# Two value steps in one run, side work at the steps between: the full-attention layers of a four-layer attention stack

## The chip, the cores and the metric

The kernel runs on one core of a Trainium2 chip. The metric is the device time of one execution in microseconds. The engines are named as in the profile: PE is TensorE (matmuls; PEld its weight loads), ACT is ScalarE, DVE is VectorE, POOL is GpSimd, SP is SyncE, from whose queue the kernel issues its DMAs.

## What is computed

Four attention layers follow each other, each with a layer norm before it and a residual sum behind it. Layers 0 and 2 look back over a window of 256 positions; layers 1 and 3 are full attention over all 2048 positions, without a mask. There are 32 heads of 16 elements.

```python
B, S, D = 1, 2048, 512
H = 32; Dh = D // H
def _B_ref(x, wqkv, wo):
    qkv = (x @ wqkv).reshape(B, S, 3, H, Dh).transpose(2, 0, 3, 1, 4)
    q, k, v = qkv[0], qkv[1], qkv[2]
    scores = jnp.einsum("bhqd,bhkd->bhqk", q, k) * Dh ** -0.5
    p = _softmax(scores, axis=-1)
    o = jnp.einsum("bhqk,bhkd->bhqd", p, v)
    return o.transpose(0, 2, 1, 3).reshape(B, S, D) @ wo

x = A_x
x = x + _A_ref(_layernorm(x), A_wqkv, A_wo)   # the same within a window of 256
x = x + _B_ref(_layernorm(x), B_wqkv, B_wo)
x = x + _A_ref(_layernorm(x), A_wqkv, A_wo)
x = x + _B_ref(_layernorm(x), B_wqkv, B_wo)
```

## The kernel before

**A step of a full layer.** The queries are cut into four chunks of 512 (c), the heads into eight groups of four (qd), the keys into sixteen tiles of 128 (j). `attn_full` (line 685) does one key tile of one head group and one chunk per step. It calls `exps` (line 642) twice, once for each pair of heads. A call takes a score buffer `s` in PSUM, fills it by two 64-row matmuls that stand side by side in the array (line 649), and has ACT take the exponential of its 128x1024 elements into a buffer `e` (line 653). There are three score buffers (pool `ps_s`, line 200) and six buffers `e` (`EB`, line 34), so six exponentials, or three steps, can be held. What I call a score tile below is one such call; a step has two.

**The values of a step** are four matmuls (line 693), one for each head, with the probabilities `e` as the moving operand and 17 columns of values (16 and a one, which gives the softmax's sum) as the stationary one. They are float32, and the profile shows each of them as two, so a step's values are eight matmuls there, in two groups of four that run side by side in the array's columns. They add up in one PSUM bank, `acc[0]`, over the sixteen steps. `attn_full` doesn't issue them itself: it hands them out as a function, which `attention` puts into the queue `pvq` and issues later with `flush` (line 656).

```python
def flush(n):
    while len(pvq) > n:
        spent(1.0)
        for f in pvq.popleft():
            f()
```

**Behind the last step of a head group** the function `epilogue` (line 591) hangs on the same queue entry: DVE copies `acc[0]` to SBUF (line 599), DMAs take it to DRAM, and two later pieces (`run_late`, line 634) take the reciprocals of the sums and normalise. The first values of the next head group write `acc[0]` again and wait for that copy.

**Side work** is everything that isn't the attention itself: projections for this layer and the next (line 385, 12 matmuls of 512 columns per output tile), the output projection, transposes for the layer norm (line 429). In a full layer it has the other bank, `acc[1]` (`bank`, line 374), and `mms` (line 380) hands it out matmul by matmul. The class `Side` (line 794) puts it in: `Side.step` (line 838) issues pieces until the share due by then is done, at most about 3 us of planned time a call, and stops behind the end of a chain of matmuls. The share due is counted in steps, and a work is taken only when a planned clock (`clock`, moved by `spent`, line 213) says that its inputs are there.

**Order.** PE follows the order in which the program is written out (`manual_schedule`), and `attention` (line 869) writes it. DVE, ACT, POOL and SP follow a scheduler. In a full layer before the change, every step writes its scores, and then `flush(2)` the values of the step two before; odd steps add side work behind them. Two steps make a unit: scores, values, scores, values, side. There are 256 units in each full layer. In a window layer every step does all three.

Of the kernel before, what the change touches and what calls it, by code (L numbers as in the profile page):

```python
# [189 lines left out]
def fast_path(ctx, tc, flag, a_x, a_wqkv, a_wo, b_wqkv, b_wo, out):  # L190
# [22 lines left out]
    def spent(us):  # L213
        clock[0] += us
        return us
# [306 lines left out]
    def settle(all_=True):  # L522
        while pend and (all_ or pend[0][0] <= clock[0]):
            pend.pop(0)[1]()
# [109 lines left out]
    def run_late(done=False):  # L634

        while late and (done or late[0][0] <= 0):
            late.popleft()[1]()
        for x in late:
            x[0] -= 1
# [16 lines left out]
# [5 lines that stand above are left out]
# [208 lines left out]
    def attention(l, works):  # L869

        win = l % 2 == 0
        PH["full"] = not win
        load = load_win if win else load_full
        for t in range(NHT if l == 3 else 1):
            for c in range(NQ):
                qds = range(2 * t, 2 * t + 2) if l == 3 else range(NQD)
                ops = load(l, c, qds[0])
                sd = Side((3 if win else NT) * len(qds) // (1 if win else 2), works[t * NQ + c], works[t * NQ + c + 1])
                k = 0
                for qd in qds:  # L880
                    nxt = load(l, c, qd + 1) if qd + 1 in qds else None
                    a = acc[qd % 2 if win else 0]
                    began = clock[0]
                    for f in (attn_win if win else attn_full)(l, c, qd, *ops, a):
                        clock[0] = max(clock[0], began + (2.4 if win else 1.8))
                        began = clock[0]
                        pvq.append([f])
                        flush(2)
                        run_late()
                        if win or k % 2:  # L890
                            sd.step()
                        if win:
                            settle(False)
                        k += 1
                    pvq[-1].append(lambda l=l, c=c, qd=qd, a=a: epilogue(l, c, qd, a, False))
                    ops = nxt
                sd.finish()
                if not win:
                    settle()
        flush(0)  # L900
        run_late(True)
        PH["full"] = False
# [122 lines left out]
    for l in range(4):  # L1025
        if l % 2 == 0:
            attention(l, works[l] + [tails[l][1:]])
            all_of(tails[l], lasts[l])
            key_shift(l + 1, 0 if l else None)
            all_of(lasts[l], works[l + 1][0])  # L1030
        else:
            attention(l, works[l] + [works[2][0] if l == 1 else [O3(3, 3)]])
# [38 lines left out]
```

## Time and profile before

| | |
|---|---|
| median of 3 runs | 2972.41 us (2970.57 to 2975.87) |
| profiled execution, its time | 2971.72 us |
| its span | 2970.0 us |
| mean granted clock of TensorE | 0.979 |
| PE busy | 2740.4 us |
| ACT busy | 2400.6 us |
| DVE busy | 904.0 us |
| POOL busy | 561.7 us |
| exponentials (line 653), all layers | 2432 instructions, 2244.0 us busy |
| values of the full layers (line 693) | 8192 matmuls in the profile, 1078.5 us busy |
| scores, all layers (line 649) | 5504 matmuls, 797.1 us busy |

A group's row gives line, engine, operation, output <- inputs, shapes and count; then busy time and the mean of one in ns; then the idle time of its engine before these instructions, and what ended it. A row of a timeline gives the start and the duration in us, the same description, and in brackets the idle time before. A row of the table by stage gives the stretch, then busy time and count of PE, PEld, DVE, ACT and POOL, the granted clock, the share of the DMA engines and GB/s. A row of the waits gives who waited for whom, the total in us, how often, and the longest. Matmuls overlap and their ends are modelled: the distance from one start to the next tells more than the duration.

### The profile page before, as it was taken

To read this page: it belongs to the slowest core of one execution; us is meant where nothing else is said; L and a number is where in the kernel's file an instruction comes from. 1 tells how busy PE (TensorE), PEld (TensorE's weight loads), DVE (VectorE), ACT (ScalarE), POOL (GpSimd) and SP (SyncE) were. 2 spreads that over 40 slices of the span, in tenths; PEclk is the share of its full clock that TensorE was granted. 3 is DMA by queue.
4 is the path that set the end of the run, shared out by engine and by line. 5 is a ranking of instruction groups with operands and counts; after the bars stand their busy time and mean duration, and the time that the engine had idled before them with its cause. 6 is when DMAs were issued, how large, how long until landed. Compare 5 with 4: busy or idle time off the path is not lost.

```text
span 2970.0 us, 52024 instructions
## 1 busy us (share of the span) xinstructions
PE 2740.4 (92%) x20314; PEld 745.7 (25%) x20314; DVE 904.0 (30%) x1914; ACT 2400.6 (81%) x2703; POOL 561.7 (19%) x1127
## 2 busy tenths in 40 slices
PE   6778889899999999999999888899999999999996
PEld 3233333321122212212212333332112211121111
DVE  7656444401113112111212455631222222222112
ACT  3454555389999999999998666639999999999996
POOL 2456564100000000000002566600000000000000
PEclk8898999999999999999999999999999999999998
DMA  6575775532223233222222756542343334333331
GB/s 212 188 227 189 237 228 172 186 107 100 77 92 104 76 115 102 92 86 93 93 102 94 228 187 184 166 135 86 127 130 123 114 126 134 123 120 122 122 114 66
DMA packets 291409, 399.35 MB, mean 134 GB/s; under 512 B 70352, under 2 KB 173264, under 8 KB 283856
## 3 DMA queue, kind: packets, MB, share of 16 engines
q1 hardware_dynamic: 291152, 395.92, 41.0%
q8 instruction: 161, 2.64, 0.4%
q14 instruction: 96, 0.79, 0.1%
HBM read 263.19 MB, written 131.60 MB: 133 GB/s over the span
## 4 chain that ended last, share of the span: by engine, by line
PE 65%; ACT 10%; DMA 10%; DVE 7%; issue 4%; POOL 2%; SPq 1%; ACTq 0%; DVEq 0%; POOLq 0%
PE acc L693 26%; PE s L649 18%; ACT e L653 9%; PE acc L385 9%; PE pq L385 4%; DMA r<-rcp 4%; PE pv L385 3%; DMA rcp<-lt 2%; PE acc L725 2%; PE po L385 2%; DMA scr<-oe 1%; POOL wr L326 1%; DMA x<-in_A_x_dram 1%; POOL w L331 1%; DVE o L626 1%
## 5 line engine op out<-in xcount | busy, mean ns | idle before, releaser
L653 ACT ACTIVATE e<-s 128x1024 f32<-128x1024 f32 (+2 forms) x2432 | 2244.0, 1113 | 173.5 <-PE s L649 156.7
L693 PE MATMUL acc<-e,vt 128*17 128x512 f32 x8192 | 1078.5, 598 | 2.8 <-DVE oe L599 2.7
L649 PE MATMUL s<-qt,kt 64*128 64x512 f16 (+3 forms) x5504 | 797.1, 356 | 88.1 <-ACT e L653 16.6
L649 PEld LDWEIGHTS <-kt 64*128 64x128 f16 x5504 | 219.1, 94 | 953.0 <-issue 928.5
L718 POOL TENSOR_SCALAR_AFFINE_SELECT e<-e 128x256 f32<-128x256 f32 x512 | 229.0, 454 | 186.4 <-ACT e L653 185.5
L599 DVE COPY oe<-acc 128x512 f32<-128x512 f32 x128 | 88.0, 687 | 510.4 <-PE acc L693 449.2
L629 POOL TENSOR_TENSOR oh<-o,oh 128x512 f16<-128x512 f32 x32 | 37.1, 1159 | 1076.6 <-DVE oh L628 1060.9
L693 PEld LDWEIGHTS acc<-e,vt 128*17 128x17 f32 x8192 | 136.4, 95 | 349.0 <-issue 322.9
L715 POOL TENSOR_SCALAR_AFFINE_SELECT e<-e 128x256 f32<-128x256 f32 x448 | 195.4, 442 | 151.1 <-ACT e L653 148.1
L385 PE MATMUL pq<-xc,w 128*128 128x512 f16 x816 | 198.3, 397 | 20.0 <-DVE dx L567 5.3
L725 PE MATMUL acc<-e,vt 128*17 128x384 f32 (+2 forms) x2816 | 203.7, 396 | 5.4 <-POOL e L715 5.3
L385 PEld LDWEIGHTS <-w 128*128 128x128 f16 x1152 | 106.5, 100 | 254.5 <-issue 161.7
L626 DVE TENSOR_TENSOR o<-o,r 128x512 f32<-128x512 f32 x64 | 51.9, 811 | 352.4 <-DMA r<-rcp 344.7
L385 PE MATMUL po<-wo,oh 128*128 128x512 f16 x444 | 113.5, 409 | 39.1 <-DVE oh L628 19.2
L461 ACT ACTIVATE sp<-pq,es 128x512 f16<-128x512 f32 x68 | 46.6, 686 | 125.5 <-PE pq L385 106.2
L469 POOL TENSOR_TENSOR sq<-sp 128x512 bf16<-128x512 f16 x28 | 29.1, 1039 | 555.8 <-DVE sp L463 555.8
L385 PE MATMUL pv<-wv,xc 128*128 128x512 f16 x576 | 129.3, 379 | 0.5 <-ACT e L653 0.5
L552 ACT ACTIVATE vt<-pv 128x512 f32<-128x512 f32 x52 | 31.1, 597 | 118.5 <-PE pv L385 118.5
L385 PEld LDWEIGHTS <-oh 128*128 128x128 f16 x768 | 68.4, 101 | 207.5 <-issue 125.0
L385 PEld LDWEIGHTS <-xc 128*128 128x128 f16 x768 | 69.8, 98 | 135.2 <-issue 62.6
L463 DVE TENSOR_SCALAR sp<-acc,es 128x512 f16<-128x512 f32 x28 | 21.0, 751 | 267.6 <-PE acc L385 231.8
L385 PE MATMUL acc<-xc,w 128*128 128x512 f16 x336 | 93.8, 383 | 3.6 <-DVE sp L464 3.6
(129 smaller groups left out, 1478.3 us busy)
## 6 DMA issues: line engine op xcount, KB each, us to landing
kt<-kf SPq DMA_DIRECT2D x128, 512.0 KB
qt<-qs SPq DMA_DIRECT2D x128, 256.0 KB
scr<-oe SPq DMA_DIRECT2D x128, 256.0 KB
xd<-x SPq DMA_DIRECT2D x96, 256.0 KB
x<-xd SPq DMA_DIRECT2D x96, 256.0 KB
w<-wd SPq DMA_DIRECT2D x22, 1024.0 KB
kt<-kw SPq DMA_DIRECT2D x64, 256.0 KB
o<-scr SPq DMA_DIRECT2D x64, 256.0 KB
```

The costliest lines, as they stand in the source:

```text
L385: nc.tensor.matmul(ps, a, b, start=(i == 0), stop=(i == len(pairs) - 1))
L461: nc.scalar.activation(sp[:, 0], ps, AF.Copy, scale=e)
L552: nc.scalar.activation(vt[:, i, :, :DH], src, AF.Copy)
L599: nc.vector.tensor_copy(oe, a)
L626: nc.vector.tensor_tensor(o, o, r, ALU.mult)
L629: (nc.gpsimd if l % 2 else nc.vector).tensor_tensor(ohl[:, 1], o, ohl[:, 0], ALU.subtract)
L649: nc.tensor.matmul(ps[:, h, s0:s0 + wd_], kt[R * h:R * h + R, pr, kc:kc + P], qt[R * h:R * h + R, pr, qc:qc + wd_], start=True, stop=True)
L653: nc.scalar.activation(e[:, :, w0:w1], ps[:, :, w0:w1], AF.Exp, scale=SCALE)
L693: nc.tensor.matmul(a[32 * h:32 * h + DH + 1, :], V[l, j // 4][:, j % 4, 4 * qd + h, :], es_[h // 2][:, h % 2, :], start=(j == 0), stop=(j ...
L715: nc.gpsimd.affine_select(v, v, pattern=[[0, 2], [-1, P]], compare_op=ALU.is_gt, fill=0.0, base=0, channel_multiplier=1)
L718: nc.gpsimd.affine_select(v, v, pattern=[[0, 2], [1, P]], compare_op=ALU.is_ge, fill=0.0, base=0, channel_multiplier=-1)
L725: nc.tensor.matmul(a[32 * h:32 * h + DH + 1, q * P:(q + nb) * P], V[l, (4 * c + j) // 4][:, j % 4, 4 * qd + h, :], es_[h // 2][:, h % 2, s ...
```

## The change

In full layers (`win` false) the values are flushed at even steps alone, down to one entry in the queue instead of two; odd steps flush none. Window layers keep `flush(2)` at each step.

```diff
                         pvq.append([f])
-                        flush(2)
+
+                        if win or k % 2 == 0:
+                            flush(2 if win else 1)
                         run_late()
                         if win or k % 2:
                             sd.step()
```

At an even step k the queue holds the values of k-2, k-1 and k, and the first two are issued, one behind the other. The step k-1 had its scores just before. So a unit becomes: scores, values of the two steps before, scores, side. The last values of a head group, and its epilogue with them, are issued at step 0 of the next group instead of step 1.

## The prediction

> **What bounds the kernel now.** I read the page first: the span, the busy shares, and the forty slices of engine use and granted clock.
>
> ```profile
> span 2970.0 us, 52024 instructions
> ...
> PE 2740.4 (92%) x20314; PEld 745.7 (25%) x20314; DVE 904.0 (30%) x1914; ACT 2400.6 (81%) x2703; POOL 561.7 (19%) x1127
> ...
> PE   6778889899999999999999888899999999999996
> ...
> ACT  3454555389999999999998666639999999999996
> ...
> PEclk8898999999999999999999999999999999999998
> ```
>
> Slices 9 to 22 and 27 to 40 are the two full layers (layers 1 and 3), and only they are edited. In both rows PE and ACT stand at 9, so the page alone doesn't say which sets the time there. The table by stage, the groups of instructions in each layer, and the timeline of ACT at the ends of each layer say more.
>
> ```profile
> 615.00:1605.00 990.00, 967.32 (x6891) 203.88 (x6892) 168.50 (x382) 949.09 (x1025) 47.46 (x46) 1.00 0.27 92
> 1987.00:2942.00 955.00, 940.09 (x6675) 190.22 (x6675) 195.09 (x358) 947.20 (x1025) 45.45 (x42) 1.00 0.36 116
> ```
>
> ```profile
> L653 ACT ACTIVATE e<-s 128x1024 f32<-128x1024 f32 x1024 | 948.6, 1159 | 40.7 <-PE s L649 39.8
> ...
> L653 ACT ACTIVATE e<-s 128x1024 f32<-128x1024 f32 x1024 | 946.7, 1117 | 7.2 <-PE s L649 6.2
> ```
>
> ```profile
> 615.53 1.02 ACT L653 ACTIVATE e<-s 128x1024 f32<-128x1024 f32 x1
> ...
> 1601.88 2.96 ACT L653 ACTIVATE e<-s 128x1024 f32<-128x1024 f32 x3
> ...
> 1987.76 1.02 ACT L653 ACTIVATE e<-s 128x1024 f32<-128x1024 f32 x1
> ...
> 2939.31 2.32 ACT L653 ACTIVATE e<-s 128x1024 f32<-128x1024 f32 x2
> ```
>
> From first to last exponential, layer 1 takes 1604.84 - 615.53 = 989.3 us and layer 3 takes 2941.63 - 1987.76 = 953.9 us. Next come the groups of score and side matmuls, and the timeline of one two-step unit with twelve side matmuls.
>
> ```profile
> L649 PE MATMUL s<-qt,kt 64*128 64x512 f16 x2048 | 334.6, 382 | 14.4 <-ACT e L653 1.0
> ...
> L385 PE MATMUL acc<-xc,w 128*128 128x512 f16 x336 | 93.8, 383 | 3.6 <-DVE sp L464 3.6
> ```
>
> ```profile
> 1203.42 0.60 PE L649 MATMUL s<-qt,kt 64*128 64x512 f16 x4
> 1203.91 3.77 ACT L653 ACTIVATE e<-s 128x1024 f32<-128x1024 f32 x4 [1.80 <-PE s L649]
> 1203.96 1.05 PE L693 MATMUL acc<-e,vt 128*17 128x512 f32 x8
> 1204.94 0.61 PE L649 MATMUL s<-qt,kt 64*128 64x512 f16 x4
> 1205.48 1.05 PE L693 MATMUL acc<-e,vt 128*17 128x512 f32 x8
> 1206.46 2.76 PE L385 MATMUL acc<-xc,w 128*128 128x512 f16 x12
> 1209.16 0.60 PE L649 MATMUL s<-qt,kt 64*128 64x512 f16 x4
> 1209.65 3.77 ACT L653 ACTIVATE e<-s 128x1024 f32<-128x1024 f32 x4 [1.97 <-PE s L649]
> ```
>
> Four exponentials from a fresh start take 3.77 us and a lone one takes 1.02, so one costs (3.77 - 1.02) / 3 = 0.917 us. A unit (four score tiles, two value steps, one side piece) therefore costs ACT 4 x 0.917 = 3.667 us, and a layer 1024 x 0.917 = 939.0 us. That floor doesn't move. Everything the change can win is the excess above it: 50.3 us in layer 1 and 14.9 us in layer 3. In this heavy unit PE sets the pace: 1209.16 - 1203.42 = 5.74 us, with ACT waiting 1.97 us. The other kind of unit, with no side work, stands at the end of layer 3, followed by three value steps in one run.
>
> ```profile
> 2936.57 0.92 PE L649 MATMUL s<-qt,kt 64*128 64x512 f16 x4
> ...
> 2937.42 1.05 PE L693 MATMUL acc<-e,vt 128*17 128x512 f32 x8
> 2938.40 0.92 PE L649 MATMUL s<-qt,kt 64*128 64x512 f16 x4
> 2938.93 0.09 PEld L649 LDWEIGHTS <-kt 64*128 64x128 f16 x1 [0.42 <-issue]
> 2939.25 0.13 PEld L693 LDWEIGHTS acc<-e,vt 128*17 128x17 f32 x8 [0.23 <-issue]
> 2939.25 3.47 PE L693 MATMUL acc<-e,vt 128*17 128x512 f32 x24
> 2939.69 0.25 PEld L693 LDWEIGHTS acc<-e,vt 128*17 128x17 f32 x4 [0.31 <-issue]
> 2940.12 0.12 PEld L693 LDWEIGHTS acc<-e,vt 128*17 128x17 f32 x4 [0.18 <-issue]
> ```
>
> Here a step takes 2938.40 - 2936.57 = 1.83 us, two exponentials. ACT sets the pace, and PE waits inside the score group: its second tile starts at 2938.93, 0.53 after the first instead of 0.22. What it waits for shows at the start of layer 1, where the fourth tile waits for the first exponential.
>
> ```profile
> 616.60 0.39 PE L649 MATMUL s<-qt,kt 64*128 64x512 f16 x2 [0.52 <-ACT e L653]
> ```
>
> That exponential ended at 615.53 + 1.02 = 616.55, and the score tile began 0.05 later. There are three score buffers, so a tile can't start before the exponential three tiles back has ended. PE's lead over ACT is capped.
>
> **The change, part by part.** It adds and removes no instruction. In the order of the built program ACT's is unchanged; DVE, POOL and SP differ by 16, 2 and 25 moved rows, all in side and epilogue work that later steps consume, which I price at nothing: DVE is busy 168.5 and POOL 47.5 of 990 us. If that cover fails, the price is of the size of the DVE waits below. On PE the order of a unit goes from scores, values, scores, values, side to scores, values, values, scores, side. No exponential buffer is lost: the six hold three steps, and no value step comes later than before.
>
> *Fewer kinds of neighbours.* Within a value step the second four-matmul group starts 0.44 after the first, and across two steps in a run 0.43 (2939.69 to 2940.12). Before scores, the last group costs 0.985 - 0.44 = 0.545, so leaving a value run costs 0.115. Scores to values take 0.535 for two tiles (1203.42 to 1203.96): the second tile comes 0.60 - 0.38 = 0.22 after the first, and values 0.31 after that. Side matmuls come (2.76 - 0.383) / 11 = 0.216 apart, and from the first of twelve to the next scores it is 2.70 (1206.46 to 1209.16), so the last takes 0.32. A unit with m side matmuls then costs PE
> - before: 2 x (0.535 + 0.985) + (0.32 - 0.216) + 0.216 m = 3.14 + 0.216 m; at m = 12 that is 5.73, against 5.74 in the rows;
> - after: 0.535 + 0.44 + 0.43 + 0.43 + 0.545 + 0.22 + (scores to side) + 0.32 + 0.216 (m - 1).
>
> Scores to side at full width has no row. Bounds: 0.216 (no price) and 0.332 (0.216 + 0.115, the largest change in the rows). I take 0.31, as scores to values, since both leave the same tile shape. That gives 3.01 + 0.216 m, 0.13 less than before.
>
> [...]
>
> *A longer run without scores.* This is the price. After the last score tile ahead of the run, PE issues no scores until both value steps are through. That tile starts at the earliest 0.05 after the exponential three tiles back. Then 0.32 to the run (2938.93 to 2939.25), 0.44 + 0.43 + 0.43 + 0.545 for the run, 0.49 from the next score tile to its exponential (1203.42 to 1203.91), and 1.02 for it: 3.725 us. ACT has three exponentials in hand when the clock starts and needs the end of the fourth at 3.667. So ACT starves 0.058 us in every unit, however little side work it has. Before, the same loop with one value step was 0.05 + 0.32 + 0.985 + 1.51 = 2.87 and left 0.8 us spare.
>
> *Sum.* A unit after costs the larger of 3.725 and 3.01 + 0.216 m, which overtakes at m = 4. Side pieces in the changed program's order: layer 3 has 244 units with m of 0 to 3, 1 with 4, 8 with 6, 3 with 7. Layer 1 has 197 (twelve with eight short transposes among them), then 35 with 4, 6 with 5, 6 with 6, one 7, one 9 and ten 12. Over the floor:
> - layer 3: 244 x 0.058 + 0.21 + 8 x 0.64 + 3 x 0.86 = 22.1 us, against 14.9 measured: +7.2.
> - layer 1: 197 x 0.058 + 35 x 0.21 + 6 x 0.42 + 6 x 0.64 + 0.86 + 1.29 + 10 x 1.935 = 46.6 us, to which come the waits that no order of PE takes away:
>
> ```profile
> PE acc L385 <- DVE sp L464: 3.6, 2, 1.8
> PE acc L693 <- DVE oe L599: 2.7, 2, 1.4
> PE acc L385 <- DVE vt L554: 1.3, 1, 1.3
> ```
>
> The middle one goes: the last values of a head group leave a step earlier, so the copy of the accumulator has one more score group and a side piece over it. The others stay, 4.9 us. Layer 1: 51.5 against 50.3, +1.2.
>
> Together +8.4 us. The profiled execution took 2971.72 us (span 2970.0), so 2980.1; the median of the runs shown is 0.7 above the profiled one. I say 2981.
>
> **The rivals.**
>
> *Break-even, 2973 us (2968 to 2977).* In layer 1 a heavy unit that follows another heavy one saves 0.13, and the unseen scores-to-side change may be free: 0.09 less in 71 units with m of 4 and more, 6.4 us. The remaining DVE waits, 4.9, may be absorbed too. Then +8.4 - 6.4 shrinks to +2, or to -3. For it: ACT's 40.7 us of idle time in layer 1. Against: layer 3, with 7.2 us idle, has little to give.
>
> *Faster, 2955 us.* PE's order alone saves 0.13 in each of the 438 units with side work, 57 us, were PE the bound in all of them; the excess over ACT's floor, 50.3 + 14.9, holds little more, and most of it sits in units that PE sets anyway. The likelier form: the fixed starvation of 0.058 is a small difference of long terms: a run 0.058 shorter than 1.845 us (leaving it at 0.487 instead of 0.545) removes it in all 441 light units, 25.6 us, and the sum is -17. [...] Against: both terms of the loop have rows, and the spread of those rows is 0.01.
>
> *Slower, about 3003 us.* The second value step of a run doesn't start at 0.43 but 0.05 late, since it needs the exponentials of the step just before, where one step's distance is left instead of two. By the loop, it starts 0.05 + 0.32 + 0.87 = 1.24 after the exponential named above, and the one that it needs ends at 0.917: 0.27 us spare. Once anything delays ACT by more than that, each 0.01 of wait costs 4.4 us over 441 units; 0.05 makes +22.
>
> *A lower clock, about 3042 us.* PE's rests before a score tile change their pattern, from two of about 0.3 us in a light unit to 0.9 us together at one place. If the granted clock fell to 0.93, the run's 1.845 would grow by 0.14, 61 us over the light units.
>
> ```profile
> 100.00:200.00 100.00, 83.22 (x643) 32.13 (x636) 52.91 (x119) 55.26 (x80) 63.50 (x119) 0.93 0.65 214
> ```
>
> That clock stood where PE was busy 83%; against it, the edited layers have 1.00 with such rests in every light unit. [...]
>
> *It does nothing it says.* The built order shows the run of two steps in all 256 units of both layers; this gets no chance.
>
> **How the numbers follow.** Chances: forecast 0.58 (its own range 2974 to 2989: the price of scores to side free, or the run's four-matmul groups all at 0.44, which adds 2 x 0.01 x 441 = 9 us), break-even 0.14, faster 0.13, slower 0.13, a lower clock 0.02. Below 0.2% (5.9 us), about what a measurement of this kernel can tell from no change, lies a quarter of the forecast, 0.14. So slower 0.44 + 0.13 + 0.02 = 0.59, same 0.14 + 0.14 = 0.28, faster 0.13. The range leaves out the lower clock, about half of faster and of slower, and the forecast's own edge: 2963 to 2998.
>
> **What would show it.** ACT in layer 3: about 961 us from first to last exponential instead of 953.9, and in layer 1 about 990. Idle time of ACT before the scores' exponentials appears in light units, once every four, some 0.06 us each. Light units last 3.72 to 3.73 us instead of 3.67. A value run of sixteen matmuls spans 1.85 us to the next scores; side work begins 0.3 us after the last score tile. The wait of the values for the copy of the accumulator is gone. The prediction is wrong if light units still take 3.67 (the loop doesn't bind), if the run is longer than 1.87, if the clock in either layer falls under 1.00, or if the difference lies outside the full layers.

## The result, and the profile after

The changed kernel took 2999.73 us (median of five runs, 2993.94 to 3006.18) against 2975.87 for the kernel before in the same set: ratio 1.0081, 95% interval 1.0064 to 1.0098, some 24 us slower. The direction was forecast, the size was not. Absolute times of the kernel before differ between the sets of runs below (medians from 2975.87 to 2986.99), so ratios are given against the kernel before of the same set, and stages are compared in the profiles.

First the page's head, and of the table by stage the full layers, 1 and 3.

```profile
span 3004.5 us, 52022 instructions
...
PE 2715.0 (90%) x20314; PEld 840.3 (28%) x20314; DVE 903.1 (30%) x1914; ACT 2422.9 (81%) x2703; POOL 560.7 (19%) x1127
```

```profile
620.00:1623.00 1003.00, 949.87 (x6894) 246.69 (x6892) 168.41 (x382) 959.99 (x1025) 47.79 (x46) 0.99 0.27 91
2010.00:2978.00 968.00, 919.81 (x6675) 236.97 (x6671) 195.23 (x358) 957.86 (x1025) 45.46 (x42) 1.00 0.35 114
```

PE has the same instructions and is busy less than the 2740.4 us of before, and the kernel is longer. ACT's first and last exponentials of each layer, from its timeline:

```profile
620.84 1.94 ACT L653 ACTIVATE e<-s 128x1024 f32<-128x1024 f32 x2
...
1620.07 1.94 ACT L653 ACTIVATE e<-s 128x1024 f32<-128x1024 f32 x2
...
2010.32 1.94 ACT L653 ACTIVATE e<-s 128x1024 f32<-128x1024 f32 x2
...
2975.25 1.94 ACT L653 ACTIVATE e<-s 128x1024 f32<-128x1024 f32 x2
```

Layer 1 takes 1622.01 - 620.84 = 1001.2 us (before 989.3), layer 3 takes 2977.19 - 2010.32 = 966.9 (before 953.9): 24.8 us more together, which is what the medians show. The span of the profiled execution grew by 34.5. The other 10 us lie outside the full layers, mainly in the window layers, whose steps are not edited. Their length scatters from profile to profile: from its first exponential to its last, layer 0 took 449.5 us before and 455.0 after, and between 450.1 and 456.6 in the ten profiles below, whichever order they have. I read nothing from them.

Light units are those that the prediction put at 3.725 us, with up to three side matmuls. One with two, in layer 3:

```profile
2501.09 0.67 PE L649 MATMUL s<-qt,kt 64*128 64x512 f16 x4
2501.68 1.91 PE L693 MATMUL acc<-e,vt 128*17 128x512 f32 x16
2503.53 0.61 PE L649 MATMUL s<-qt,kt 64*128 64x512 f16 x4
2504.07 0.61 PE L385 MATMUL acc<-xc,w_h 128*128 128x512 f16 x2
2504.60 0.88 PE L649 MATMUL s<-qt,kt 64*128 64x512 f16 x4
2505.41 1.05 PE L693 MATMUL acc<-e,vt 128*17 128x512 f32 x8
```

From one value run to the next it is 2505.41 - 2501.68 = 3.73 us, where ACT needs 3.667. The run takes 2503.53 - 2501.68 = 1.85 to the next scores. The loop binds as drawn in the prediction. Between the ends of the same exponential in neighbouring units I measured, as medians by the number m of side matmuls in the unit:

| m | forecast, us | measured, us |
|---|---|---|
| 0 to 3 | 3.725 | 3.731 |
| 4 | 3.87 | 3.886 |
| 6 | 4.31 | 4.320 |
| 7 | 4.52 | 4.532 |
| 12 | 5.60 | 5.612 |

Two things stand outside this table. The first is in the waits of PE in layer 1, and in a timeline of one of them:

```profile
PE acc L385 <- DVE sp L464: 5.1, 2, 2.6
PE acc L385 <- DVE vt L554: 4.8, 2, 2.5
```

```profile
1065.13 0.61 PE L649 MATMUL s<-qt,kt 64*128 64x512 f16 x4
...
1065.62 0.69 DVE L626 TENSOR_TENSOR o<-o,r 128x512 f32<-128x512 f32 x1 [8.24 <-DMA r<-rcp]
1066.35 0.43 DVE L628 CAST oh<-o 128x512 f16<-128x512 f32 x1
1066.69 0.74 DVE L463 TENSOR_SCALAR sp<-acc,es 128x512 f16<-128x512 f32 x1
...
1067.47 0.75 DVE L464 SCALAR_TENSOR_TENSOR sp<-acc,es,sp 128x512 f16<-128x512 f32 x1
...
1068.27 1.88 PE L385 MATMUL acc<-xc,w 128*128 128x512 f16 x6 [2.53 <-DVE sp L464]
...
1070.08 1.03 PE L649 MATMUL s<-qt,kt 64*128 64x512 f16 x4
1070.79 1.94 ACT L653 ACTIVATE e<-s 128x1024 f32<-128x1024 f32 x2 [3.23 <-PE s L649]
...
1071.05 2.64 PE L693 MATMUL acc<-e,vt 128*17 128x512 f32 x16
```

DVE starts its instructions here in the order of its queue. It waits 8.24 us for the reciprocals' DMA, and behind that stand the two copies (lines 463 and 464) that free the accumulator of the side work. The side matmuls wait 2.53 us, and the scores wait behind them on PE. Then the same score group takes 1.03 us instead of 0.61, and the value run 2.64 instead of 1.91. The granted clock of these stretches shows why:

```profile
1066.00:1069.00 3.00, 0.73 (x4) 0.37 (x4) 2.15 (x4) 1.56 (x2) 2.08 (x2) 1.00 0.13 44
1069.00:1072.50 3.50, 3.50 (x16) 0.58 (x18) 0.00 (x0) 1.71 (x2) 0.07 (x1) 0.52 0.71 226
1072.50:1076.00 3.50, 3.50 (x31) 0.82 (x25) 0.00 (x0) 2.12 (x4) 0.00 (x0) 0.99 0.01 6
```

The clock was halved for one stretch of 3.41 us. Layer 1 has three such stretches; before it had none.

In the order of before, the same place looked like this:

```profile
1054.74 0.75 DVE L463 TENSOR_SCALAR sp<-acc,es 128x512 f16<-128x512 f32 x1 [4.71 <-PE acc L385]
...
1058.16 0.69 DVE L626 TENSOR_TENSOR o<-o,r 128x512 f32<-128x512 f32 x1 [2.66 <-DMA r<-rcp]
1058.77 0.74 DVE L464 SCALAR_TENSOR_TENSOR sp<-acc,es,sp 128x512 f16<-128x512 f32 x1
1059.42 0.42 DVE L628 CAST oh<-o 128x512 f16<-128x512 f32 x1
```

There the first copy ran ahead of the DMA wait and the cast (line 628) behind the second copy. In the changed kernel both stand between the multiply and the second copy: from the multiply's start to the release it takes 2.60 us instead of 1.35.

The second is an exponential of layer 3 that starts late behind its scores:

```profile
2041.52 0.60 PE L649 MATMUL s<-qt,kt 64*128 64x512 f16 x4
...
2042.29 1.94 ACT L653 ACTIVATE e<-s 128x1024 f32<-128x1024 f32 x2 [0.24 <-PE s L649]
```

It is 0.77 us from scores to exponential instead of 0.49. This happens sixteen times, once every sixteen units of layer 3, and in no unit of layer 1.

### The profile page after: what moved, and what is told of

Read it like the earlier page. It is cut to its first block, busy times and chain, and to the rows that moved or that the text cites. A ratio compares the mean times of both kernels' runs of the same rounds, so it can differ in the third digit from the quotient of the medians.

```text
span 3004.5 us, 52022 instructions
## 1 busy us (share of the span) xinstructions
PE 2715.0 (90%) x20314; PEld 840.3 (28%) x20314; DVE 903.1 (30%) x1914; ACT 2422.9 (81%) x2703; POOL 560.7 (19%) x1127
## 3 DMA queue, kind: packets, MB, share of 16 engines
q8 instruction: 161, 2.64, 0.4%
## 4 chain that ended last, share of the span: by engine, by line
PE 53%; ACT 22%; DMA 8%; DVE 7%; issue 5%; POOL 3%; SPq 1%; ACTq 0%; DVEq 0%; POOLq 0%
ACT e L653 22%; PE acc L693 19%; PE s L649 15%; PE acc L385 7%; PE pq L385 4%; PE pv L385 3%; DMA r<-rcp 3%; PE acc L725 2%; DMA rcp<-lt 2%; PE po L385 2%; DMA scr<-oe 1%; POOL wr L326 1%; POOL w L331 1%; DMA x<-in_A_x_dram 1%; DVE o L626 1%
## 5 line engine op out<-in xcount | busy, mean ns | idle before, releaser
L693 PE MATMUL acc<-e,vt 128*17 128x512 f32 x8192 | 983.1, 597 | 0.0
L649 PE MATMUL s<-qt,kt 64*128 64x512 f16 (+3 forms) x5504 | 810.8, 358 | 149.4 <-ACT e L653 93.6
L693 PEld LDWEIGHTS acc<-e,vt 128*17 128x17 f32 x8192 | 227.1, 96 | 413.5 <-issue 388.1
L461 ACT ACTIVATE sp<-pq,es 128x512 f16<-128x512 f32 x68 | 46.6, 686 | 127.8 <-PE pq L385 109.0
```

The lines of the kernel that those rows point to most:

```text
L461: nc.scalar.activation(sp[:, 0], ps, AF.Copy, scale=e)
L649: nc.tensor.matmul(ps[:, h, s0:s0 + wd_], kt[R * h:R * h + R, pr, kc:kc + P], qt[R * h:R * h + R, pr, qc:qc + wd_], start=True, stop=True)
L693: nc.tensor.matmul(a[32 * h:32 * h + DH + 1, :], V[l, j // 4][:, j % 4, 4 * qd + h, :], es_[h // 2][:, h % 2, :], start=(j == 0), stop=(j ...
```

## The experiments

Three questions: whether the loop of scores and value run is what sets light units, or the number of changes of kind on PE and its total work; where layer 1's extra came from; and what the late exponentials of layer 3 are. All lengths of layers are from the first exponential to the last, each from one profile.

**Side work behind the run.** The rival of the loop is that PE's work and its changes of kind set the time. Moving the side work to the even steps saves one more change and puts all of it into the loop.

```diff
-                        if win or k % 2:
+                        if win or k % 2 == 0:
                             sd.step()
```

> The changed order, but side work stands at the even steps, behind the run of two value steps: scores, values, values, side, scores. The loop theory (ACT starves because PE has no score tile to give it from the last tile ahead of the run until the first one behind it) expects that each side matmul now lengthens the loop of 3.73 us by 0.216 us, from the first one on: some 1220 matmuls in the 438 units with side work, so about 260 us more than the changed kernel, 3250 to 3270 us in all. The rival, that the number of changes of kind on PE and its total work set the time, expects a little less than the changed kernel, since the unit has three changes instead of four: 2960 to 3000 us.

Measured: 3262.06 us in one run, layers at 1120.3 and 1094.1 us, 246 us more than the changed kernel in the two. The unit of layer 3 grows with each side matmul, from 3.73 us with none to 4.05, 4.27 and 4.49 with one, two and three. The order with the fewest changes is the slowest by far. The rival's 2960 to 3000 is out.

**Shorter value runs, in both kernels.** A dose of the loop itself: the value matmuls of odd key tiles over 448 or 480 of 512 queries.

```diff
+                w = QC if j % 2 == 0 else 448
                 for h in range(4):
-                    nc.tensor.matmul(a[32 * h:32 * h + DH + 1, :], V[l, j // 4][:, j % 4, 4 * qd + h, :],
-                                     es_[h // 2][:, h % 2, :], start=(j == 0), stop=(j == NT - 1),
+                    nc.tensor.matmul(a[32 * h:32 * h + DH + 1, :w], V[l, j // 4][:, j % 4, 4 * qd + h, :],
+                                     es_[h // 2][:, h % 2, :w], start=(j == 0), stop=(j == NT - 1),
```

> The changed order, with the value matmuls of every odd key tile in full layers run over 448 of the 512 queries only, so the sums of 64 queries miss half of the key tiles. A run of two value steps is 0.107 us shorter. The loop theory expects the loop to fall from 3.731 to 3.624 us, below ACT's 3.667, so light units return to 3.667 us, no shorter, and heavy units lose 0.107 us each: 441 x 0.065 + 71 x 0.107 = 36 us, and the 16 delays of 0.28 us in layer 3 may vanish (4 us). In all 2955 to 2967 us. The rival, that PE's total work counts, expects 512 x 0.107 = 55 us less, with light units at 3.62: not possible below ACT's rate, so light units are the test.

> The changed order with the value matmuls of odd key tiles over 480 of 512 queries, so the sums of 32 queries miss half of the key tiles; half the dose of the 448 run. The loop theory expects the loop at 3.731 - 0.053 = 3.678 us and so light units at 3.678 us, between the 3.731 of the changed kernel and the 3.667 of the 448 run; layer 3 at about 954 us (966.9 - 244 x 0.053). If ACT's rate or the number of changes set light units, they do not follow the dose: 3.667 or 3.731.

> The kernel before, with the same shortening of the odd key tiles' value matmuls to 448 queries. The loop theory expects that only units which PE sets gain: none of the units with up to two side matmuls, those with three or more about 0.1 us each, together 12 to 19 us, so 2953 to 2962 us. If PE's total work counts in every unit, it gains as much as the changed kernel does from the same edit, 36 us or more: 2936 us or less.

Two neighbouring value runs in light units, with 448 queries and then with 480, from the timelines of PE:

```profile
2500.39 1.80 PE L694 MATMUL acc<-e,vt 128*17 128x512 f32 x16
...
2504.05 1.80 PE L694 MATMUL acc<-e,vt 128*17 128x512 f32 x16
```

```profile
2501.46 1.86 PE L694 MATMUL acc<-e,vt 128*17 128x512 f32 x16
...
2505.14 1.05 PE L694 MATMUL acc<-e,vt 128*17 128x512 f32 x8
```

They are 3.66 and 3.68 us apart; the median light unit took 3.667 and 3.680 us. So light units follow the dose (3.731, 3.680) until ACT's own rate holds them, and stop there. Neither ACT's rate nor the number of changes would put the 480 run between the two. Layer 3 took 953.6 us with 480 queries (954 expected) and 948.7 with 448; its sixteen late exponentials, which might have gone, stayed. In the order of before, units with up to two side matmuls stood at 3.667 with and without the edit, and the 104 units of layer 3 with three went from a median of 3.756 to 3.667. The ratios to the kernel before are 0.9941 (0.9922 to 0.996) for the changed order with 448 queries and 0.9925 (0.9897 to 0.9953) for the order of before with 448, that is -1.4% against the changed kernel's 1.0081 and -0.75% against 1. The full layers lost 40.7 us in the one (1968.0 to 1927.3) and 17.5 in the other (1943.2 to 1925.7). 36 to 40 and 12 to 19 were expected.

**Normalising on POOL.** If side matmuls wait because DVE stands at the reciprocals' DMA, the multiply that waits for it can go to POOL, with the two instructions behind it.

```diff
-                nc.vector.tensor_tensor(o, o, r, ALU.mult)
+                eng = nc.gpsimd if l % 2 else nc.vector
+                eng.tensor_tensor(o, o, r, ALU.mult)
...
-                nc.vector.tensor_copy(ohl[:, 0], o)
-                (nc.gpsimd if l % 2 else nc.vector).tensor_tensor(ohl[:, 1], o, ohl[:, 0], ALU.subtract)
+                eng.tensor_copy(ohl[:, 0], o)
+                eng.tensor_tensor(ohl[:, 1], o, ohl[:, 0], ALU.subtract)
```

> The changed order, but in full layers the two normalising steps that wait for the reciprocals' DMA (the product o times r and its cast) run on POOL instead of DVE, so DVE isn't held up ahead of the copies that free the side work's accumulator. The cover theory (side matmuls now follow the scores directly, the 0.985 us of a value step no longer stand over the copy, PE waits about 2.5 us four times in layer 1, and after three of them the clock is granted at half for 3.4 us) expects the waits of side matmuls for DVE in layer 1 to fall from 9.9 us to under 2, no half clock in that layer, and layer 1 about 13 to 15 us shorter, 986 to 988 us from first to last exponential; layer 3 stays at 967. In all 2983 to 2990 us. If the waits have another cause, they stay and the time does not move.

> The kernel before with the two normalising steps of full layers on POOL instead of DVE. Its layer 1 has 5 to 6 us of side matmuls waiting for copies that stand behind a DMA wait on DVE. The cover theory expects these to go: layer 1 at 983 to 984 us instead of 989.3, layer 3 unchanged at 953.9, 5 us less in all (ratio to the kernel before about 0.998), against some 15 us that the same edit gave the changed kernel. If the edit is worth the same in both, the cover is not what differs.

> The changed order with the normalising steps on POOL, as measured above, beside the same kernel of before on this chip, for a closer interval: full layers 1954 us, 10.6 us more than the 1943.2 of before, ratio 1.003 to 1.005.

With the changed order, PE's waits in layer 1, the layer's row in the table by stage, and its first and last exponential:

```profile
PE s L650 <- ACT e L654: 37.3, 84, 0.6
PE pq L385 <- ACT e L654: 1.0, 1, 1.0
```

```profile
622.00:1609.00 987.00, 943.66 (x6888) 245.91 (x6887) 154.73 (x352) 959.74 (x1025) 75.74 (x76) 1.00 0.28 92
```

```profile
622.17 1.02 ACT L654 ACTIVATE e<-s 128x1024 f32<-128x1024 f32 x1
...
1607.71 1.02 ACT L654 ACTIVATE e<-s 128x1024 f32<-128x1024 f32 x1
```

The waits of side matmuls for DVE are gone, the clock is 1.00 throughout, and layer 1 takes 986.6 us, 14.6 less; layer 3 stays at 967.2. The ratio falls from 1.0081 to 1.0033 (1.0018 to 1.0048), and on another set 1.0028 (1.0015 to 1.0042). In the order of before the same edit takes layer 1 from 989.3 to 984.0, 5.3 us, and the ratio of 0.999 (0.9973 to 1.0006) can't be told from 1. So in these profiles the waits in the DVE queue, with the half clock behind them, cost the changed kernel 9.3 us more than the kernel before. The size scatters: the four units concerned took 14.9 us more than their number of side matmuls allows in the changed kernel, and 10.4 to 12.4 in the three other runs that have its order and normalise on DVE (448 queries, 480 queries, one ACT instruction), with one or two half clocks in layer 1 instead of three.

These runs show that the waits go by DVE's queue, and not why they are longer in the changed order: whatever delays that queue goes with it to POOL. The theory of lost cover, which both expectations name, has to be held against the traces of the two kernels. They show something else. The chain that DVE waits for starts with the copy of `acc[0]` (line 599) and goes through three transfers (lines 604, 617 and 623). The table counts in us from that copy on, to the moment when PE has nothing left ahead of the side matmuls, and to the end of the copy that frees their accumulator:

| the four places in layer 1 | side matmuls ready, before and after, us | accumulator free, before and after, us |
|---|---|---|
| values (line 554), first | 15.46, 15.99 | 16.73, 18.40 |
| values (line 554), second | 15.46, 15.98 | 14.94, 18.27 |
| projections (line 464), first | 11.23, 11.82 | 12.92, 14.30 |
| projections (line 464), second | 11.23, 11.82 | 13.01, 14.36 |

The side matmuls come 0.5 to 0.6 us later, so they gained cover. The accumulator comes free 1.3 to 3.3 us later. For the projections 1.25 us of that is DVE's order, shown above. For the values it is mainly SP's queue: ahead of the reciprocals' transfer (line 617) it stands at line 622, which waits until the transfer of line 605 has landed. The second place, first before and then after, from SP's timelines:

```profile
1236.61 0.33 SPq L369 DMA_DIRECT2D w<-wd  x1
...
1240.40 0.58 SPq L604 DMA_DIRECT2D lt<-oe  x1
1241.04 0.45 SPq L605 DMA_DIRECT2D scr<-oe  x1
1244.48 0.62 SPq L622 DMA_DIRECT2D o<-scr  x1
```

```profile
1247.52 0.40 SPq L369 DMA_DIRECT2D w<-wd  x1
1248.60 0.58 SPq L604 DMA_DIRECT2D lt<-oe  x1
1249.24 0.45 SPq L605 DMA_DIRECT2D scr<-oe  x1
1255.68 0.63 SPq L622 DMA_DIRECT2D o<-scr  x1
```

From line 605 to line 622 it takes 6.44 us instead of 3.44, and 6.76 instead of 5.62 at the first place. The epilogue's transfers now leave 1.08 us behind a transfer of 1024 KB of weights (line 369) instead of 3.79. That the weights' transfer slows them is inferred from this distance, over all profiles (last section); no run moved that transfer alone.

**One more ACT instruction at the start.**

```diff
+            if l == 2:
+                dummy = vp.tile([P, 1], F32, name="dummy", tag="dummy", bufs=1)
+                nc.scalar.activation(dummy, onesf[:, 0:1], AF.Copy)
```

The scheduler put it at the head of the program: it runs at 2.1 us.

> The changed kernel with one tiny activation (128x1) more at its start, so that every later ACT instruction stands one place further in the stream. Sixteen times in layer 3, 128 ACT instructions apart, the first exponential behind a value run starts 0.77 us after its scores instead of 0.49, and an instruction transfer follows each time within a microsecond. If the delay belongs to the place in ACT's instruction stream, it leaves that exponential: no unit of 4.01 us in layer 3, and layer 3 takes about 962.5 us instead of 966.9. If it belongs to the change of head group (the accumulator's copy, the next loads), which falls on the same units, nothing changes: sixteen units of 4.01 us, 966 to 967 us.

```profile
1995.84 1.02 ACT L653 ACTIVATE e<-s 128x1024 f32<-128x1024 f32 x1
...
2957.69 1.02 ACT L653 ACTIVATE e<-s 128x1024 f32<-128x1024 f32 x1
```

Layer 3 takes 2958.71 - 1995.84 = 962.9 us, 4.0 less, and none of the sixteen units has 4.01 us any more. One instruction of 128 elements, almost 2000 us earlier, moved the delay. It belongs to the place in the instruction stream, not to the change of head group.

**A shorter side piece in the order of before**, on top of the normalising on POOL. There PE's own time says what side work costs: by the prediction's 3.14 + 0.216 m, nothing up to two matmuls in a unit and 3.79 us against ACT's 3.667 with three. The expectation put three at nothing; the kernel before has 104 such units in layer 3, with a median of 3.756 us.

```diff
-            while self.q and self.spent < due and self.spent - s0 < 3:
+            while self.q and self.spent < due and self.spent - s0 < ((0.6 if due - s0 < 5 else 0.8) if PH["full"] else 3):
```

> The kernel before with the normalising steps on POOL, and with side pieces in full layers of at most 3 matmuls a unit (4 while more than 5 us of planned work is behind) instead of up to 12. The loop theory says that in the order of before a piece costs nothing up to three matmuls and 0.216 us a matmul beyond: the eleven units of layer 3 with six and seven matmuls and the ten of layer 1 with twelve lose their price, against 87 units with four at 0.1 to 0.15 us and two long pieces at the end of a chunk. Layer 3 at 946 to 949 us, layer 1 at 978 to 982, together 13 to 17 us less than before: ratio 0.994 to 0.996. If side pieces cost the same wherever they stand, only the POOL part remains, 0.998.

Half of it came. Layer 3 took 948.1 us, as expected, but layer 1 took 987.7. Its 87 units with four matmuls mostly follow each other and take 4.01 us each, PE's own time (3.14 + 4 x 0.216 = 4.00), not the 0.1 to 0.15 over 3.667 that was expected; and the two long pieces cost 6.5 us each. The ratio is 0.9979 (0.9965 to 0.9993). So the last run keeps layer 1 as it was.

```diff
...
-        PH["full"] = not win
+        PH["full"], PH["piece"] = not win, 0.6 if l == 3 else 3
...
-            while self.q and self.spent < due and self.spent - s0 < 3:
+            while self.q and self.spent < due and self.spent - s0 < PH["piece"]:
```

> The kernel before with the normalising steps on POOL, and with side pieces of at most 3 matmuls in layer 3 alone; layer 1 keeps its pieces of up to 12. The run with short pieces in both layers lost in layer 1 what it won in layer 3: 87 units with four matmuls in a row at 4.01 us. The loop theory expects the sum of the two parts measured there: layer 1 at 984 us (as with POOL alone), layer 3 at 948 us, 11 us less than before in the full layers, ratio 0.995 to 0.997. If the pieces of layer 3 and layer 1 depend on each other, layer 1 is longer than 986.

```profile
1992.64 1.02 ACT L654 ACTIVATE e<-s 128x1024 f32<-128x1024 f32 x1
...
2939.31 1.39 ACT L654 ACTIVATE e<-s 128x1024 f32<-128x1024 f32 x1
```

Layer 3 takes 2940.70 - 1992.64 = 948.1 us and layer 1 takes 984.0; the two parts add up. The ratio is 0.9968 (0.9954 to 0.9982): this version beats both kernels, with the order of before.

## Why the prediction was right and wrong

It forecast slower, by 8.4 us, with the starving loop as the cause; it was slower by 25 us, of which the loop and PE's order made about half and two things that the sum held at nothing the rest. The time fell just above the range. By the profiles of the full layers, with the experiments as the dividing lines:

| term | forecast, us | measured, us | from |
|---|---|---|---|
| order of PE alone (loop, heavy units) | 8.8 | 11.9 | both kernels with POOL: 1953.8 - 1937.9, less the late exponentials' 4 |
| side matmuls waiting for DVE, with the half clock | -0.4 | 9.3 | 14.6 gained by POOL after, 5.3 before |
| late exponentials | 0 | 4 | one ACT instruction: 966.9 to 962.9 |
| sum | 8.4 | 25.2 | 1968.0 - 1943.2 = 24.8 |

The forecasts of the first two rows come from the prediction's sum by the same division: 22.1 + 46.6 over the floor, less 14.9 and the 45.0 (984.0 - 939.0) that layer 1 of before has without its waits; and 4.9 us of waits against 5.3.

- *A longer run without scores* held. The loop was put at 3.725 us and measured 3.731. The 0.006 and ACT's rate, nearer 3.666 than 3.667, make the starvation 0.065 us a unit instead of 0.058, and over 441 light units that is the 3 us by which the first term is off. A small difference of two long times was the right reason to keep a wide range.
- *Scores to side* had no row. I took 0.31; it is 0.31 to 0.32 (2503.53, plus 0.22 for the second tile, to 2504.07). The bound of no price was wrong, and with it *Break-even*.
- The step that failed is the price of the moved rows: "DVE, POOL and SP differ by 16, 2 and 25 moved rows, all in side and epilogue work that later steps consume, which I price at nothing", and with it "The others stay, 4.9 us" in *the sum for layer 1*. The reason given was that DVE and POOL are little busy. But the side matmuls wait for the end of a chain through DVE and the DMA queue, and there the order counts. The waits grew from 4.9 to 9.9 us: by DVE's order for the projections, and for the values by transfers that land later and hold up SP's queue, as the table under *Normalising on POOL* shows. The sentence "If that cover fails, the price is of the size of the DVE waits below" named the right size, but it didn't enter the sum.
- For the values the order is what differs: their waits took 3.7 to 4.8 us in the four profiles of the changed order that normalise on DVE, and 1.3 and 0 in the two of the order of before. For the projections that is less sure: 4.4 to 5.3 us in the changed order, but 3.6 and 5.1 in the order of before (the 5.1 in the run with 448 queries). The prediction asked for cover at the accumulator of the attention, which gained it as it said (its 2.7 us of waits are gone).
- The same step hid the clock, which fell to 0.99 in layer 1 and was one of the prediction's signs of being wrong. Three of the four longer waits were followed by a half clock of 3.41 us. The four units took 14.9 us more than their m allows, of which 9.9 is the waits: some 5 us is the clock. The rival of a lower clock had 0.02 and looked for it at the rests before a score tile, which are short (0.6 us at most in layer 1 of the changed kernel); it came behind the long waits, which the sum held fixed; the longest wait of PE that the prediction shows is 1.8 us. The waits of 2.33, 2.53 and 2.59 us were followed by a half clock, the one of 2.46 us was not, so their length alone doesn't tell them apart; no run shows what else decides.
- *The late exponentials* are no term of the sum. The prediction looked at ACT's order, which doesn't change, and not at where in that order an exponential without stock would stand: 4 us.
- *Faster* (fewer changes) is refuted by the side work behind the run: the fewest changes and the longest time. PE was indeed busy less, 2715.0 us instead of 2740.4, and it was no use, since ACT's next scores were behind the run. *Slower, about 3003 us* named a time close to the one measured for a reason that did not occur, so that would have been luck: the second step of a value run follows the first at 0.43 us in 507 of 510 runs, and the other three (0.74 to 0.85) stand at half clock.

## What to carry to other kernels

When two engines feed each other through a few buffers, write down the loop from the last buffer handed over to the next one, and put each proposed run into it: time saved on one engine counts for nothing if the run is longer than what the other holds in stock (here PE was busy 25.4 us less, and the two layers took 24.8 us more). When work is moved on one engine, compare the order of the other queues too, as built: a wait that a profile shows is the end of a chain through several of them, a moved row in that chain can have a price even if its engine is mostly idle (here 1.25 us at each of two places, with DVE busy 168 of 1003 us), and a transfer that leaves earlier may leave right behind a large one (here 1.08 us behind 1024 KB, instead of 3.79). A queue that waits in order for a DMA is best cleared first: here that edit was worth 5 us in one order and 15 in the other.

## What the runs showed of the hardware

- In the full layers of the twelve profiles, of 15 pauses of PE of 2.1 to 2.8 us, 9 were followed by one stretch of 3.41 us at half clock, which begins 2 to 4 us after PE stopped. Of 33 pauses of 1.0 to 1.9 us, 1 was.
- In layer 1 of the twelve profiles, where line 622 stands right behind line 605 in SP's queue: when the transfer of line 605 (256 KB) was issued 1.6 to 1.7 us behind a transfer of weights (line 369, 1024 KB), line 622 followed it after 5.9 to 6.9 us (twelve cases); 4.3 to 5.1 us behind, after 3.3 to 5.6 (ten cases); 6.8 to 8.5 us behind, after 2.2 to 2.3 us (all of 23 cases). The transfers of keys that go out just before them may have a share.
- The late exponentials of layer 3 stand 128 ACT instructions apart (semaphore waits counted), and a transfer of the queue that the profile calls instruction follows each within 0.6 to 0.9 us; the profile counts 96 of them with 0.79 MB, 8.2 KB each. The delay is 0.28 us where ACT has nothing in stock: it is idle for 0.24 to 0.25 us ahead of each of the sixteen. In the kernel before, where ACT's order is the same, the same sixteen places have a transfer 0.5 to 1.3 us behind and no idle time of ACT ahead, so the delay doesn't show. That the transfers are the cause is inferred from the spacing and from the shift by one instruction; no run changed the transfers themselves.
